# Second matmul's seven-product scheme with shared sums, and the second value pass of an attention pair begun with its shared last rows

## The chip, the cores and the metric

One NeuronCore of one Trainium2 chip runs the whole program. The metric is device time in microseconds: the median of three runs. The profile is one further execution, taken with the hardware profiler.

## The reference

```python
# q, k, v: (8 batches, 12 heads, 448 tokens, 64), float32
scores = q @ k.T / sqrt(64)
attn = exp(scores - max);  attn = attn / sum(attn)
x = (attn @ v) as (8*448 = 3584 tokens, 12*64 = 768)
h = x @ w_in            # w_in: 768 x 2048
g = h * sigmoid(h)      # silu
out = g @ w_out         # w_out: 2048 x 768 -> 3584 x 768 float32
```

## The kernel before

**Attention.** The twelve heads of a batch are three groups of four (HG = 4). A unit is one group of one batch; batch 0 is cut into two pieces of tokens. Seven units are worked alone, the other 20 as ten pairs (`ns` has two entries). A unit's keys are four chunks; in a pair the first three chunks have 128 rows each and the fourth has 64 rows of either unit, so that both units share one exponential tile, `E[(ns[0], 3)]`: its rows 0 to 63 are the first unit's last keys, rows 64 to 127 the second's. TensorE makes the scores (line 327, tile geometry 32 rows x 128 columns, in the shared chunk 32 x 64), ScalarE the exponentials (line 364), and TensorE multiplies by the values in two passes, `attend(ns, 1)` and `attend(ns, 2)` (line 390), one for each half of the head's 64 channels. Geometry there is 128 x 32, four heads side by side; for the shared chunk, called the rest, it is 64 x 32, eight matmuls side by side. Each pass of a pair is seven steps: three for each unit, and then the rest. The sums of the exponentials are part 0 (`attend_sums`, line 406). VectorE's `norm` (line 473) divides and frees the two banks of a pass.

**First matmul.** `ffn1` (line 487) makes h in 16 blocks of 128 hidden units for a batch; ScalarE's tanh (line 498) and VectorE's gate (line 534) make G. The last two batches go together through a seven-product scheme of their own (`pair_product`, line 623, with sums on VectorE at lines 581 and 599), which the change leaves alone.

**Second matmul.** The 28 tiles of 128 tokens are 14 quads of two tiles, a and b. The first quad is done plainly (line 709). Each of the other 13 is a 2 x 2 block product: rows are the two token tiles, the inner dimension is the two halves of the hidden units, columns the two halves of 768. Seven products of eight 128x128x384 matmuls (line 695) take the place of eight. `combine_w` (line 524) makes sums of w_out's quarters once, in halves; `combine_g` (line 685) makes five sums of G's quarters for each quad, in two halves each, into S tiles (a ring of NSG) or in place; `product(qd, m)` runs one product; two products may share a PSUM bank, the second added on top of the first after the first has been read. The readers are ScalarE copies (lines 753, 759, 763) and VectorE adds (line 749) of 128x384 float32, with temporaries `s` and `m` (a ring of NTMP) and output tiles `ost` (a ring of four). `store` sends an output tile out as four DMAs of 48 KB, from SP; in the last two quads two of the four go from ScalarE. `tmp`, `s`, `m`, `u` and `ost` are in SBUF; `a`, `h`, `p`, `f` and `o` banks share a ring of four PSUM banks (tag "m").

**Order.** Nothing is ordered by hand. A planner (`Order`, `run_av`, `queue_quad`, the loop at the end) walks through modelled time with a cost for each operation, and picks for TensorE the next of scores, value passes and the list `moe` whose inputs, banks and ring places are free; VectorE and ScalarE take the ready operation with the smallest due time. The program is emitted in that order, and each engine then runs its own instructions strictly in it. `SWITCH` is the planner's price for a change of TensorE's tile geometry:

```python
SWITCH = 0.094
    def on_pe(self, op, mode):
        gap = SWITCH if mode != self.mode else 0.0
```

A product's `deps()` name what must be done before it, and a ring's `take` and `give` stand for buffers; `STORE = 3.0` is the planner's time from the last write of an output tile until it is free again.

Of the kernel before, what the change touches and what calls it, by code (L numbers as in the profile page):

```python
# [165 lines left out]
def kernel(  # L166
# [41 lines left out]
    NSG, NTMP, NOST = 3, 3, 4  # L208
# [11 lines left out]
    zeros = const.tile([128, 128], FP16, name="zeros")  # L220
    nc.vector.memset(zeros, 0.0)
    ones = const.tile([128, 32], FP16, name="ones")
    nc.vector.memset(ones, 1.0)
    half = const.tile([128, 2, 32], FP16, name="half")
    nc.vector.memset(half, 0.0)
    for i in range(2):
        nc.vector.memset(half[:, i, 16 * i : 16 * (i + 1)], 1.0)
# [170 lines left out]
    def attend_sums(ns):  # L398
        a = ps.tile([128, 512], FP32, name=f"a_{ns[0]}_0", tag="m", bufs=4)
        for n in ns:  # L400
            acc[(n, 0)] = a
        for i, (w, e) in enumerate(
            ((half[:, 0], T[ns[0]]), (half[:, 1], T[ns[1]]), (both, E[(ns[0], 3)]))
        ):
            for h in range(HG):
                nc.tensor.matmul(  # L406
                    out=a[32 * h : 32 * (h + 1), 0:S],
                    lhsT=w,
                    rhs=e[:, h, 0:S],
                    start=(i == 0),  # L410
                    stop=(i == 2),
                )

    def attend(ns, part):
        made = []
        lone = len(ns) == 1
        if part == 0 and not lone:
            attend_sums(ns)
            return
        for n in ns:  # L420
            a = ps.tile([128, 512], FP32, name=f"a_{n}_{part}", tag="m", bufs=4)
            made.append(a)
            acc[(n, part)] = a
# [84 lines left out]
    W_ = {m: const.tile([128, HF, OH], FP16, name=f"D{m}") for m in (1, 4, 6)}  # L508
# [5 lines left out]
    W_[3], W_[7], W_[5], W_[2] = B_[0, 1], B_[1, 0], B_[1, 1], B_[0, 0]  # L514

    def combine_w(m, f0, f1):
        i0, i1, op = {
            1: ((0, 0), (1, 1), ALU.add),
            4: ((1, 0), (0, 0), ALU.subtract),
            6: ((0, 0), (0, 1), ALU.add),  # L520
            3: ((0, 1), (1, 1), ALU.subtract),
            7: ((1, 0), (1, 1), ALU.add),
        }[m]
        nc.vector.tensor_tensor(
            out=W_[m][:, f0:f1], in0=B_[i0][:, f0:f1], in1=B_[i1][:, f0:f1], op=op
        )
# [129 lines left out]
    def first_silu():  # L656
        t = const.tile([128, 1], FP16, name="first_silu")
        nc.scalar.activation(out=t, in_=zeros[:, 0:1], func=AF.Silu)
# [11 lines left out]
    def combine_g(qd, m, f0, f1):  # L670
        a, b = 2 * qd, 2 * qd + 1
        x, y, op = {
            5: (rows(a, 0), rows(a, 1), ALU.add),
            2: (rows(b, 0), rows(b, 1), ALU.add),
            1: (rows(a, 0), rows(b, 1), ALU.add),
            6: (rows(b, 0), rows(a, 0), ALU.subtract),
            7: (rows(a, 1), rows(b, 1), ALU.subtract),
        }[m]
        if m > 5:
            dst = x  # L680
# [4 lines left out]
        nc.vector.tensor_tensor(out=dst[:, f0:f1], in0=x[:, f0:f1], in1=y[:, f0:f1], op=op)  # L685

    BANK = {3: 3, 5: 3, 4: 4, 2: 4, 1: 1, 7: 1, 6: 6}

    def product(qd, m):
        w = {3: rows(2 * qd, 0), 4: rows(2 * qd + 1, 1), 6: rows(2 * qd + 1, 0), 7: rows(2 * qd, 1)}  # L690
# [34 lines left out]
    def tmp(qd, name):  # L725
        tmp_t[(qd, name)] = sb.tile([128, OH], FP32, name=f"{name}_{qd}", tag="tmp", bufs=NTMP)
        return tmp_t[(qd, name)]
# [24 lines left out]
    def take_3(qd):  # L752
        nc.scalar.copy(out=tmp(qd, "s"), in_=bank(qd, 3))

    def take_4(qd):
        add(tmp_t[(qd, "s")], bank(qd, 4), tmp_t[(qd, "s")])

    def take_5(qd):
        nc.scalar.copy(out=ost(qd, 0, 1), in_=bank(qd, 3))  # L759
        store(qd, 0, 1)  # L760

    def take_2(qd):
        nc.scalar.copy(out=ost(qd, 1, 0), in_=bank(qd, 4))  # L763
        store(qd, 1, 0)

    def take_1(qd):
        add(tmp(qd, "m"), bank(qd, 1), tmp_t[(qd, "s")])

    def less_12(qd):
        add(tmp_t[(qd, "s")], tmp_t[(qd, "s")], ost_t[(qd, 0, 1)], ALU.subtract)  # L770

    def less_21(qd):
        add(tmp_t[(qd, "m")], tmp_t[(qd, "m")], ost_t[(qd, 1, 0)], ALU.subtract)

    def take_6(qd):
        add(ost(qd, 1, 1), bank(qd, 6), tmp_t[(qd, "m")])
        store(qd, 1, 1)

    def take_7(qd):
        add(ost(qd, 0, 0), bank(qd, 1), tmp_t[(qd, "s")])  # L780
        store(qd, 0, 0)
# [104 lines left out]
    pr_op, sg_op, w_op, plain_op = {}, {}, {2: [], 5: []}, {}  # L886
# [3 lines left out]
    def queue_ffn1(b, g0, g1):  # L890
        t0, t1 = 32 * g0, 32 * g1
        for f in range(NFF) if b == 0 else [x for f in range(HF) for x in (f, f + HF)]:
# [22 lines left out]
            def deps(f=f):  # L915
# [3 lines left out]
                for qd in range(NT * B // 4) if u else ():  # L919
                    if any(t // NT == u - 1 and (r or t % NT < 4) for t in (2 * qd, 2 * qd + 1)):  # L920
                        made += (
                            [plain_op.get(x) for x in ((0, 0), (0, 1), (1, 0), (1, 1))]
                            if qd == 0
                            else [pr_op.get((qd, m)) for m in (3, 4, 6, 7)]
                        )
# [55 lines left out]
    def queue_pair_f(f, xs):  # L981
        done, lo = {}, f // 4 * 4

        def free(r):
            made = []
            for qd in range(NT * B // 4):
                for t in (2 * qd, 2 * qd + 1):
                    if t // NT == PB // 2 - 1 and t % NT < (4, NT - 1)[r]:
                        made += [pr_op.get((qd, m)) for m in (3, 4, 6, 7)]
# [68 lines left out]
    def sums_w(ms):  # L1058

        for m in ms:  # L1060
            w_op[m] = [
# [5 lines left out]
                        ld_wout + list(plain_op.values()) * (m in (3, 7)),  # L1067
# [6 lines left out]
    def queue_plain(t, j):  # L1074
# [6 lines left out]
        def queue(f0, f1):  # L1081
            def run():
# [10 lines left out]
                if len(plain_op) == 4:  # L1093
                    sums_w((3, 7))
# [22 lines left out]
    def plan_sums():  # L1117
# [12 lines left out]
        for m in (5, 2, 1, 6, 7):  # L1130
            sg_op[(qd, m)] = []
            for f0 in (0, 4):
                deps = [x for f in range(f0, f0 + 4) for x in gates[f] + gates[f + HF]]
                if m > 5:
                    deps += sg_op[(qd, {6: 2, 7: 5}[m])]
# [12 lines left out]
    def queue_quad(qd):  # L1148
# [3 lines left out]
        def read(m, eng, fn, deps, then=None):  # L1152
            if m in (5, 2):
                then = lambda at: (m_ring.give(at), ost_ring.give(at + STORE))
            elif m in (6, 7):
                then = lambda at: (
                    m_ring.give(at), ost_ring.give(at + STORE), tmp_ring.give(at)
                )
# [4 lines left out]
        def queue(m, first):  # L1163
            def run():
# [5 lines left out]
                if m in (5, 2, 1):  # L1170
# [3 lines left out]
                if m == 3:  # L1174
                    read(3, "ACT", take_3, [op])
                elif m == 4:
                    read(4, "DVE", take_4, [op, took[3]])
                elif m == 5:
                    read(5, "ACT", take_5, [op], m_ring.give)
                elif m == 2:  # L1180
                    read(2, "ACT", take_2, [op], m_ring.give)
                elif m == 1:
                    read(1, "DVE", take_1, [op, took[4]])
                    read("less_12", "DVE", less_12, [took[1], took[5]])
                    read("less_21", "DVE", less_21, [took[1], took[2]])
                elif m == 6:
                    read(6, "DVE", take_6, [op, took["less_21"]], m_ring.give)
                else:
                    read(7, "DVE", take_7, [op, took["less_12"]], m_ring.give)

            def deps():
                made = list(w_op.get(m, [None])) + [x for y in first if y for x in [took.get(y)]]
                if m in (3, 4):
                    t = 2 * qd + m - 3
                    for b in {(128 * t + c) // S for c in (0, 127)}:
                        for f in range(HF):
                            x = g_op.get((b, f + HF * (m - 3)), [None])
                            made += [(y, f * mm(OH)) for y in x]
                    return made + ld_wout
                if m in (1, 6, 7):  # L1200
                    made += [pr_op.get((qd, x)) for x in ((5, 2) if m == 1 else (1,))]
# [3 lines left out]
            rings = {3: ((tmp_ring, 1),), 1: ((tmp_ring, 1),), 4: ()}  # L1205
            rings = rings.get(m, ((ost_ring, 1),))
            moe.append((deps, 1 if BANK[m] == m else 0, run, rings))


        for m, first in ((3, ()), (4, (3,)), (5, (3,)), (2, (4,)), (1, ()), (6, ()), (7, (1,))):  # L1210
            queue(m, first)

    def after_x(n):
# [16 lines left out]
        if b == 0:  # L1230
            sums_w((1, 4, 6))
# [153 lines left out]
    def run_av():  # L1385
# [27 lines left out]
        od.on_pe(op, "cols")  # L1413
        if two and part:
            od.mode = "rest cols"
# [140 lines left out]
```

## Time and profile before

| | |
|---|---|
| median of 3 runs | 395.43 us (395.18 to 395.46) |
| the profiled execution's own time | 395.72 us |
| its span | 393.9 us |
| TensorE | 386.8 us busy, 98% of the span, 3679 matmuls |
| VectorE | 311.0 us, 79%, 653 instructions |
| ScalarE | 243.1 us, 62%, 378 instructions |
| granted TensorE clock | 1.00 |
| second matmul's sums of G, line 685 | 130 instructions, about 0.42 us each |
| its reading adds on VectorE, line 749 | 78 instructions, about 0.55 us each |
| its copies on ScalarE, lines 753, 759, 763 | 39 instructions, 0.48 us each |
| sums of w_out, line 524 | 10 instructions, about 0.94 us each |
| stores, line 744 | 224 DMAs of 48 KB, median 1.7 us from issue to landing |

A matmul's duration in the profile includes its way through the array, and matmuls overlap; how long one holds TensorE is read from the distance between starts. The same holds in part for VectorE and ScalarE, whose next instruction can begin before the last one's end.

### The profile page before, as it was taken

The page shows a single profiled execution, that of the slowest core. Times are in us where ns is not written, and L with a number is a line of the kernel's source. Part 1 is how long each engine was busy: PE and PEld are TensorE (multiplying, and loading weights), DVE is VectorE, ACT ScalarE, POOL GpSimd, SP SyncE. Part 2 cuts the span into 40 slices and gives each one's busy share as a digit, 9 for nine tenths or more (in the row PEclk, how much of TensorE's full clock was granted, in tenths as well). Part 3 has the DMA queues.
Part 4 walks back from the last instruction along what each step waited for, and adds up shares of the span by engine and source line. Part 5 has one row for each costly group of instructions (what it writes and reads, how often), then busy time and mean ns, then how long its engine had stood idle before and what let it go on. Part 6 is the DMA issues. An engine that isn't in the chain of part 4 may idle for free.

```text
span 393.9 us, 9299 instructions
## 1 busy us (share of the span) xinstructions
PE 386.8 (98%) x3679; PEld 199.3 (51%) x3679; DVE 311.0 (79%) x653; ACT 243.1 (62%) x378; POOL 83.7 (21%) x153
## 2 busy tenths in 40 slices
PE   7999999999999999999999999999999999999995
PEld 6667774443444444544444444344444555556563
DVE  2476676999999697896888886988879898786863
ACT  4988885696863878626868529687593227872110
POOL 6632447205003232500051221500000000000000
PEclk9999999999999999999999999999999999999999
DMA  7999999919034863582134861801100131001334
GB/s 112 203 210 210 164 177 185 162 35 142 0 71 95 140 95 47 77 157 70 25 48 78 143 108 47 119 2 42 42 1 2 40 81 40 2 1 42 80 82 121
DMA packets 35580, 34.44 MB, mean 87 GB/s; under 512 B 11600, under 2 KB 34000, under 8 KB 35536
## 3 DMA queue, kind: packets, MB, share of 16 engines
q0 software_dynamic: 24784, 22.82, 38.7%
q1 hardware_dynamic: 9984, 10.24, 9.5%
q10 hardware_dynamic: 768, 0.79, 0.8%
q8 instruction: 29, 0.48, 0.5%
q14 instruction: 15, 0.12, 0.1%
HBM read 45.61 MB, written 11.01 MB: 144 GB/s over the span
## 4 chain that ended last, share of the span: by engine, by line
PE 96%; DMA 1%; ACT 1%; issue 0%; DVE 0%; POOL 0%; POOLq 0%
PE p L695 31%; PE h L487 29%; PE s L327 13%; PE a L390 10%; PE f L623 8%; PE o L709 3%; PE a L406 2%; DMA rq<-in_q_dram 1%; PE z L1463 1%; ACT E L364 1%; POOL rk L248 0%; DVE ost L749 0%; ACT ost L763 0%; DVE rq L314 0%; ACT th L498 0%
## 5 line engine op out<-in xcount | busy, mean ns | idle before, releaser
L364 ACT ACTIVATE E<-s 128x896 f16<-128x896 f32 (+1 forms) x172 | 149.9, 915 | 48.9 <-PE s L327 47.7
L487 PE MATMUL h<-xT,w_in_t 128*128 128x448 f16 (+1 forms) x672 | 118.5, 327 | 0.0
L487 PEld LDWEIGHTS <-w_in_t 128*128 128x128 f16 x672 | 61.2, 98 | 54.1 <-issue 18.0
L498 ACT ACTIVATE th<-h 128x448 f16<-128x448 f32 (+1 forms) x112 | 54.2, 494 | 31.4 <-PE h L487 22.5
L534 DVE SCALAR_TENSOR_TENSOR G<-th,h 128x448 f16<-128x448 f16 (+2 forms) x112 | 55.4, 509 | 16.0 <-ACT th L498 13.7
L269 POOL DMA_DIRECT2D V<-in_v_dram x88 | 48.6, 571 | 57.4 <-PE a L390 43.8
L327 PE MATMUL s<-rq,KT 32*128 32x448 f16 (+4 forms) x864 | 56.7, 340 | 1.4 <-DVE rq L314 0.9
L695 PEld LDWEIGHTS <-G 128*128 128x128 f16 x384 | 36.5, 98 | 28.1 <-issue 4.4
L695 PEld LDWEIGHTS <-S 128*128 128x128 f16 x312 | 29.3, 98 | 23.8 <-issue 5.2
L390 PE MATMUL a<-E,V 128*32 128x448 f16 (+3 forms) x864 | 40.4, 335 | 0.0
L695 PE MATMUL p<-D,G 128*128 128x384 f16 x208 | 37.6, 326 | 0.0
L695 PE MATMUL p<-w_out_t,S 128*128 128x384 f16 x208 | 37.1, 326 | 0.0
L254 POOL DMA_DIRECT2D rq<-in_q_dram x27 | 15.2, 561 | 103.2 <-PE s L327 83.8
L473 DVE SCALAR_TENSOR_TENSOR xT<-a,rdn 128x448 f16<-128x448 f32 (+1 forms) x54 | 28.8, 567 | 7.3 <-PE a L390 6.4
L327 PEld LDWEIGHTS <-KT 32*128 32x128 f16 (+2 forms) x864 | 17.5, 98 | 29.5 <-issue 26.0
L695 PE MATMUL p<-w_out_t,G 128*128 128x384 f16 x176 | 31.9, 326 | 0.0
L390 PEld LDWEIGHTS <-V 128*32 128x32 f16 (+2 forms) x864 | 18.2, 95 | 22.4 <-issue 14.7
L375 DVE TENSOR_TENSOR T<-T,E 128x1792 f16<-128x1792 f16 x20 | 21.8, 1090 | 8.3 <-ACT E L364 8.1
L685 DVE TENSOR_TENSOR S<-G 128x512 f16<-128x512 f16 x70 | 25.4, 416 | 3.2 <-PE p L695 3.0
L375 DVE TENSOR_TENSOR T<-E,E 128x1792 f16<-128x1792 f16 x20 | 21.7, 1084 | 5.8 <-ACT E L364 5.8
L759 ACT COPY ost<-p 128x384 f32<-128x384 f32 x13 | 6.2, 480 | 26.9 <-PE p L695 22.1
L304 DVE STREAM_TRANSPOSE KT<-rk 128x256 f32<-128x256 f32 (+3 forms) x48 | 16.6, 384 | 6.4 <-DMA rk<-in_k_dram 5.7
(72 smaller groups left out, 364.1 us busy)
## 6 DMA issues: line engine op xcount, KB each, us to landing
out_dram<-ost SPq DMA_DIRECT2D x208, 48.0 KB, 1.7
rk<-in_k_dram POOLq DMA_DIRECT2D x24, 224.0 KB, 5.7
rq<-in_q_dram POOLq DMA_DIRECT2D x21, 224.0 KB, 5.2
w_in_t<-in_moe_w_in_dram POOLq DMA_DIRECT2D x6, 512.0 KB, 11.4
w_out_t<-in_moe_w_out_dram POOLq DMA_DIRECT2D x4, 768.0 KB, 12.9
V<-in_v_dram POOLq DMA_DIRECT2D x43, 64.0 KB, 3.9
V<-in_v_dram POOLq DMA_DIRECT2D x40, 48.0 KB, 3.8
out_dram<-ost ACTq DMA_DIRECT2D x16, 48.0 KB, 1.8
```

What stands on the lines that cost most here:

```text
L269: nc.gpsimd.dma_start(out=VT[b][32 * x : 32 * (x + 1), hs, 0:count, :], in_=v[b, hs].rearrange("h (i g) d -> i h g d", g=TPP)[:, :, first ...
L327: nc.tensor.matmul(out=pS[p0 : p0 + 32 * (x1 - x0), h % 2, at : at + nq], lhsT=KT[(b, hg)][32 * h : 32 * (h + 1), c, x0:x1, :, e], rhs=QT[ ...
L364: nc.scalar.activation(out=E[(n, w)][0:kr, 2 * y : 2 * y + 2, 0:nk], in_=pS_t[(n, w, y)][0:kr, :, 0:nk], func=AF.Exp, scale=attn_scale,)
L375: nc.vector.tensor_tensor(out=T[n], in0=T[n] if step else E[(n, 0)], in1=E[(n, step + 1)], op=ALU.add,)
L390: nc.tensor.matmul(out=a[32 * h : 32 * (h + 1), 0:nq], lhsT=w, rhs=e[k0:k1, h, at : at + nq], start=start, stop=stop,)
L473: nc.vector.scalar_tensor_tensor(out=x3(b, cc)[:, cc % 3, 32 * g0 : 32 * g1], in0=acc[(n, part)][:, 0:nq], scalar=0.5, in1=rdn_t[n].rearra ...
L487: nc.tensor.matmul(out=h[:, 0 : t1 - t0], lhsT=w_in_t[:, cc, 128 * f : 128 * (f + 1)], rhs=x3(b, cc)[:, cc % 3, t0:t1], start=(cc == 0), s ...
L498: nc.scalar.activation(out=th, in_=h_t[(b, f, t0)][:, 0 : t1 - t0], func=AF.Tanh)
L534: nc.vector.scalar_tensor_tensor(out=dst[:, f, at + lo : at + hi], in0=th_t[(b, f, t0)][:, lo - t0 : hi - t0], scalar=1.0, in1=h_t[(b, f, ...
L623: nc.tensor.matmul(out=pp_t[(f, PBANK[m])], lhsT=w[:, c, :], rhs=a[:, c, :], start=(c == 0 and m in (1, 6, 5, 7)), stop=(c == 2), skip_gro ...
L685: nc.vector.tensor_tensor(out=dst[:, f0:f1], in0=x[:, f0:f1], in1=y[:, f0:f1], op=op)
L695: nc.tensor.matmul(out=pr_t[(qd, BANK[m])][:, 0:OH], lhsT=w[:, f, :], rhs=W_[m][:, f, :], start=(f == 0 and BANK[m] == m), stop=(f == HF - 1),
```

## The change

1. The seven products are those of another scheme. With a, b the token tiles and 0, 1 the halves: S5 = b0 + b1, S6 = S5 - a0, in place b0 := a0 - b0 (for product 7), S3 = a1 - S6; four sums for each quad instead of five, in a chain. Weights: four sums instead of five, also a chain (B11 - B01, + B00, then B10 less that, and in place B01 - B00). Products run in the order 1, 6, 2, 7, 5, 4, 3 instead of 3, 4, 5, 2, 1, 6, 7. Bank 1 takes products 1 and 2, bank 7 products 7 and 4, bank 5 products 5 and 3, product 6 has its own.
2. The readers: ScalarE copies product 1 into `u` and bank 1 (with product 2) out; VectorE makes five adds, all of which read a bank. It was three ScalarE copies and six adds, of which two read SBUF alone.
3. NSG is 4 instead of 3, NTMP 2 instead of 3; `zeros` lies in an S tile, `half` and `ones` are views of one tile, `first_silu` writes into a `th` tile.
4. In a pair, part 2 begins with the rest (64 x 32) and then runs the three chunks of either unit (128 x 32); part 1 still ends with the rest. The planner's mode follows.

Core of the diff (resource declarations and ring bookkeeping cut):

```diff
-    NSG, NTMP, NOST = 3, 3, 4
+    NSG, NTMP, NOST = 4, 2, 4
...
     def attend(ns, part):
...
+        def rest():
+            for h in range(HG):
+                for i, n in enumerate(ns):
+                    attend_mm(
+                        acc[(n, part)], n, part, 3, h, 64 * i, 64 * (i + 1), E[(ns[0], 3)],
+                        part == 2, part == 1,
+                    )
+
+        if part == 2 and not lone:
+            rest()
+        for n in ns:
             for c in range(NCH if lone else NCH - 1):
                 for h in range(HG):
                     attend_mm(
-                        a, n, part, c, h, 0, rows_of(n, c), E[(n, c // per_burst(n))],
-                        c == 0, lone and c == NCH - 1,
+                        acc[(n, part)], n, part, c, h, 0, rows_of(n, c),
+                        E[(n, c // per_burst(n))],
+                        c == 0 and (lone or part == 1),
+                        c == NCH - 1 or (c == NCH - 2 and not lone and part == 2),
                     )
-        if not lone:
-            for h in range(HG):
-                for i, n in enumerate(ns):
-                    attend_mm(
-                        made[i], n, part, 3, h, 64 * i, 64 * (i + 1), E[(ns[0], 3)],
-                        False, True,
-                    )
+        if part == 1 and not lone:
+            rest()
...
-            1: ((0, 0), (1, 1), ALU.add),
-            4: ((1, 0), (0, 0), ALU.subtract),
-            6: ((0, 0), (0, 1), ALU.add),
-            3: ((0, 1), (1, 1), ALU.subtract),
-            7: ((1, 0), (1, 1), ALU.add),
+            3: (B_[1, 1], B_[0, 1], ALU.subtract),
+            2: (W_[7], B_[0, 0], ALU.add),
+            4: (B_[1, 0], W_[6], ALU.subtract),
+            1: (B_[0, 1], B_[0, 0], ALU.subtract),
...
-            5: (rows(a, 0), rows(a, 1), ALU.add),
-            2: (rows(b, 0), rows(b, 1), ALU.add),
-            1: (rows(a, 0), rows(b, 1), ALU.add),
-            6: (rows(b, 0), rows(a, 0), ALU.subtract),
-            7: (rows(a, 1), rows(b, 1), ALU.subtract),
+            5: (rows(b, 0), rows(b, 1), ALU.add),
+            6: (S_t.get((qd, 5)), rows(a, 0), ALU.subtract),
+            7: (rows(a, 0), rows(b, 0), ALU.subtract),
+            3: (rows(a, 1), S_t.get((qd, 6)), ALU.subtract),
...
-    BANK = {3: 3, 5: 3, 4: 4, 2: 4, 1: 1, 7: 1, 6: 6}
+    BANK = {1: 1, 2: 1, 6: 6, 7: 7, 4: 7, 5: 5, 3: 5}
...
+    def take_1(qd):
+        nc.scalar.copy(out=tmp(qd), in_=bank(qd, 1))
+    def take_2(qd):
+        nc.scalar.copy(out=ost(qd, 0, 0), in_=bank(qd, 1))
+        store(qd, 0, 0)
+    def take_6(qd):
+        add(tmp_t[qd], bank(qd, 6), tmp_t[qd])
+    def take_7(qd):
+        add(ost(qd, 1, 1), bank(qd, 7), tmp_t[qd])
+    def take_5(qd):
+        add(ost_t[(qd, 1, 1)], bank(qd, 5), ost_t[(qd, 1, 1)])
+        store(qd, 1, 1)
+    def take_4(qd):
+        add(ost(qd, 1, 0), bank(qd, 7), tmp_t[qd])
+        store(qd, 1, 0)
     def take_3(qd):
-        nc.scalar.copy(out=tmp(qd, "s"), in_=bank(qd, 3))
...
+        add(ost(qd, 0, 1), bank(qd, 5), tmp_t[qd])
         store(qd, 0, 1)
...
+                made += [took.get(y) for y in {2: (1,), 4: (7,), 3: (5,)}.get(m, ())]
+                made += [(pr_op.get((qd, y)), 9.0) for y in {6: (1,), 7: (6,), 5: (7,), 3: (4,)}.get(m, ())]
...
-        for m, first in ((3, ()), (4, (3,)), (5, (3,)), (2, (4,)), (1, ()), (6, ()), (7, (1,))):
-            queue(m, first)
+        for m in (1, 6, 2, 7, 5, 4, 3):
+            queue(m)
...
-        od.on_pe(op, "cols")
+        od.on_pe(op, "rest cols" if two and part == 2 else "cols")
         if two and part:
-            od.mode = "rest cols"
+            od.mode = ("rest cols", "cols")[part - 1]
```

More of the change, by code (lines that the diff above doesn't have):

```diff
@@ L218 @@
     )
-    zeros = const.tile([128, 128], FP16, name="zeros")
+    zeros = sb.tile([128, NFF // 2, 128], FP16, name="zeros", tag="S", bufs=NSG)[:, 0]
     nc.vector.memset(zeros, 0.0)
-    ones = const.tile([128, 32], FP16, name="ones")
+    cols = const.tile([128, 64], FP16, name="cols")
+    ones, half = cols[:, 16:48], (cols[:, 32:64], cols[:, 0:32])
+    nc.vector.memset(cols, 0.0)
     nc.vector.memset(ones, 1.0)
[L224 to L227, printed above, removed]
     both = const.tile([128, 32], FP16, name="both")
@@ L402, in attend_sums @@
         for i, (w, e) in enumerate(
-            ((half[:, 0], T[ns[0]]), (half[:, 1], T[ns[1]]), (both, E[(ns[0], 3)]))
+            ((half[0], T[ns[0]]), (half[1], T[ns[1]]), (both, E[(ns[0], 3)]))
         ):
@@ L420, in attend @@
         for n in ns:
-            a = ps.tile([128, 512], FP32, name=f"a_{n}_{part}", tag="m", bufs=4)
-            made.append(a)
-            acc[(n, part)] = a
+            acc[(n, part)] = ps.tile([128, 512], FP32, name=f"a_{n}_{part}", tag="m", bufs=4)
+        def rest():
[8 more added lines that the diff above has]
+        for n in ns:
             for c in range(NCH if lone else NCH - 1):
@@ L507 @@
     X = const.tile([128, NFF, 128], FP16, name="X")
-    W_ = {m: const.tile([128, HF, OH], FP16, name=f"D{m}") for m in (1, 4, 6)}
+    W_ = {m: const.tile([128, HF, OH], FP16, name=f"D{m}") for m in (2, 3, 4)}
     B_ = {
@@ L656, in first_silu @@
     def first_silu():
-        t = const.tile([128, 1], FP16, name="first_silu")
-        nc.scalar.activation(out=t, in_=zeros[:, 0:1], func=AF.Silu)
+        t = sb.tile([128, S], FP16, name="first_silu", tag="th", bufs=3)[:, 0:1]
+        nc.scalar.activation(out=t, in_=both[:, 0:1], func=AF.Silu)
     def silu(f, r, x):
@@ L723, in bank, with tmp @@
         return pr_t[(qd, m)][:, 0:OH]
-    def tmp(qd, name):
-        tmp_t[(qd, name)] = sb.tile([128, OH], FP32, name=f"{name}_{qd}", tag="tmp", bufs=NTMP)
-        return tmp_t[(qd, name)]
+    def tmp(qd):
+        tmp_t[qd] = sb.tile([128, OH], FP32, name=f"u_{qd}", tag="tmp", bufs=NTMP)
+        return tmp_t[qd]
     def ost(qd, i, j):
@@ L749, in add @@
         nc.vector.tensor_tensor(out=out, in0=a, in1=b, op=op)
-    def take_3(qd):
-        nc.scalar.copy(out=tmp(qd, "s"), in_=bank(qd, 3))
[L755 to L759, printed above, removed]
-        store(qd, 0, 1)
[L762 to L781, printed above, removed]
+    def take_1(qd):
[13 more added lines that the diff above has]
+        store(qd, 1, 0)
+    def take_3(qd):
+        add(ost(qd, 0, 1), bank(qd, 5), tmp_t[qd])
+        store(qd, 0, 1)
     units = []
@@ L923, in deps @@
                             if qd == 0
-                            else [pr_op.get((qd, m)) for m in (3, 4, 6, 7)]
+                            else [pr_op.get((qd, m)) for m in (1, 2, 4, 7)]
                         )
@@ L988, in free @@
                     if t // NT == PB // 2 - 1 and t % NT < (4, NT - 1)[r]:
-                        made += [pr_op.get((qd, m)) for m in (3, 4, 6, 7)]
+                        made += [pr_op.get((qd, m)) for m in (1, 2, 4, 7)]
             return made
@@ L1060, in sums_w @@
         for m in ms:
-            w_op[m] = [
+            out = {1: 5, 2: 6, 3: 7, 4: 4}[m]
+            w_op[out] = [
                 od.add(
@@ L1066, in sums_w @@
                         lambda m=m, f0=f0: combine_w(m, f0, f0 + 4),
-                        ld_wout + list(plain_op.values()) * (m in (3, 7)),
+                        ld_wout
+                        + [w_op[x][f0 // 4] for x in {2: (7,), 4: (6,)}.get(m, ())]
+                        + list(plain_op.values()) * (m == 1),
                         30,
@@ L1129, in plan_sums @@
         sg_ring.take(3)
-        for m in (5, 2, 1, 6, 7):
+        for m in (5, 6, 7, 3):
             sg_op[(qd, m)] = []
@@ L1161, in read, with out, both, queue @@
             took[m] = od.add(Op(eng, busy, lambda: fn(qd), deps, bias, then=then))
-        def queue(m, first):
+        def out(at):
+            ost_ring.give(at + STORE)
+        def both(*rings):
+            return lambda at: [m_ring.give(at), out(at)] + [r.give(at) for r in rings]
+        def queue(m):
             def run():
@@ L1173, in run @@
                 pr_op[(qd, m)] = op
-                if m == 3:
-                    read(3, "ACT", take_3, [op])
-                elif m == 4:
[L1177 to L1187, printed above, removed]
+                if m == 1:
+                    read(1, "ACT", take_1, [op])
+                elif m == 6:
+                    read(6, "DVE", take_6, [op, took[1]], m_ring.give)
+                elif m == 2:
+                    read(2, "ACT", take_2, [op], both())
+                elif m == 7:
+                    read(7, "DVE", take_7, [op, took[6]])
+                elif m == 5:
+                    read(5, "DVE", take_5, [op, took[7]], out)
+                elif m == 4:
+                    read(4, "DVE", take_4, [op, took[6]], both())
@@ L1188, in run @@
                 else:
-                    read(7, "DVE", take_7, [op, took["less_12"]], m_ring.give)
+                    read(3, "DVE", take_3, [op, took[4]], both(tmp_ring))
             def deps():
-                made = list(w_op.get(m, [None])) + [x for y in first if y for x in [took.get(y)]]
-                if m in (3, 4):
-                    t = 2 * qd + m - 3
+                made = list(w_op.get(m, [None]))
+                made += [took.get(y) for y in {2: (1,), 4: (7,), 3: (5,)}.get(m, ())]
@@ L1199, in deps @@
                     return made + ld_wout
-                if m in (1, 6, 7):
-                    made += [pr_op.get((qd, x)) for x in ((5, 2) if m == 1 else (1,))]
                 x = sg_op.get((qd, m), [None, None])
                 return made + [x[0], (x[1], 4 * mm(OH))]
-            rings = {3: ((tmp_ring, 1),), 1: ((tmp_ring, 1),), 4: ()}
-            rings = rings.get(m, ((ost_ring, 1),))
-            moe.append((deps, 1 if BANK[m] == m else 0, run, rings))
-        for m, first in ((3, ()), (4, (3,)), (5, (3,)), (2, (4,)), (1, ()), (6, ()), (7, (1,))):
-            queue(m, first)
+            rings = {1: ((tmp_ring, 1),), 2: ((ost_ring, 1),), 7: ((ost_ring, 1),)}
@@ L1213, in after_x @@
+            rings.update({4: ((ost_ring, 1),), 3: ((ost_ring, 1),)})
+            rings = rings.get(m, ())
+            moe.append((deps, int(BANK[m] == m), run, rings))
+        for m in (1, 6, 2, 7, 5, 4, 3):
+            queue(m)
     def after_x(n):
```

38 lines of the change are left out of this document (16 added, 22 removed).

## Prediction

> **What bounds the kernel now.** I read the page first, then TensorE's waits, then the chain of waits in order of time, then the timeline around the two places where TensorE stood still beside the changed code, and last the output tiles' own view.
>
> ```profile
> span 393.9 us, 9299 instructions
> PE 386.8 (98%) x3679; PEld 199.3 (51%) x3679; DVE 311.0 (79%) x653; ACT 243.1 (62%) x378; POOL 83.7 (21%) x153
> ...
> PE 96%; DMA 1%; ACT 1%; issue 0%; DVE 0%; POOL 0%; POOLq 0%
> ```
>
> TensorE carries 96% of the chain. VectorE's 79% and ScalarE's 62% are not the bound, so work taken off them counts only where TensorE waits for them. All of TensorE's waits:
>
> ```profile
> PE z L1463 <- DVE zeros L221: 1.0, 1, 1.0
> PE s L327 <- DVE rq L314: 0.9, 1, 0.9
> PE p L695 <- ACT ost L763: 0.6, 1, 0.6
> PE s L327 <- ACT E L364: 0.4, 1, 0.4
> PE a L390 <- issue: 0.2, 1, 0.2
> ```
>
> Only the third lies in code that the change touches. So the time is nearly the sum of TensorE's steps, and the chain shows what a step costs:
>
> ```profile
> 75.91 2.27 PE h L487 x12
> ...
> 78.69 2.38 PE h L487 x12
> ...
> 120.90 3.13 PE a L390 x61
> 124.03 1.41 PE p L695 x8
> ...
> 156.16 1.30 PE p L695 x8
> ```
>
> Columns are start, length, what. Twelve h matmuls take 2.27 us behind work of the same tile geometry (0.189 each) and 2.38 behind scores: a change of geometry costs about 0.1. A product is 1.30 without, 1.41 with. The two value passes of a pair, back to back, are 14 steps of 0.189, or 2.65, yet take 3.13: four changes (128x32 to 64x32, back, again, and out) are the other 0.48. (x61 for 64: a few records are missing.)
>
> **The geometry changes.** The matmul count stays 3679 with the same shapes, so the steps cost the same. I counted the changes over the two built orders: 258 before, 251 after. A change's price is the distance from a step's first start to the next step's first start in this trace, less the step's own columns (0.187 for 448: the 0.189 above, of which 0.002 is what every step adds); within a kind it varies by a few ns. By kind, with C for 128x32, R for the 64x32 rest, F for full 128x128, S for the scores' 32x128:
>
> - C to R, 20 to 10, at 0.106: -1.06. R to F, 13 to 4, at 0.129: -1.16. F to C, 13 to 6, at 0.096: -0.67. S to F, 59 to 56, at 0.109: -0.33.
> - C to F, 12 to 22, at 0.108: +1.08. R to C, 6 to 10, at 0.127: +0.51. S to C, 28 to 31, at 0.105: +0.32.
> - New kinds: F to R, 5, for which the trace has no row; the nearest are F to the scores' 32x64 step at 0.096 and C to R at 0.106, so +0.48 to +0.53. R to R across two passes, 5, no change of geometry; bounds are C to C at 0.003 and one 32x64 step behind another at 0.041 (eight staggered starts, which is the nearer row), so +0.02 to +0.20; a gain below nothing is excluded, since no step is shorter than its columns.
>
> Sum -0.58 to -0.82; with 0.096 and 0.03 for the new kinds it is -0.69. Only five of the ten pairs have their passes back to back in the new order; for the others the change moves a geometry change from one pass to the other.
>
> The Trainium skill (TensorEngine Tiling (Array Packing), Tiling Modes) says that changing the tiling mode, but not merely the tile, drains TensorE; it gives no price. The trace agrees for mode changes, with 0.096 to 0.129; no row here yet shows R to R. If the drain were the 128 cycles that the skill's TensorE: Matmul & The Clock Gate (Part 2) names, an estimate of 0.053 us at 2.4 GHz, seven changes fewer would be 0.37 us instead of 0.69, and the time 394.8.
>
> Beginning part 2 with the rest needs both accumulators at its first step instead of the second one three steps (0.57) later. The planner takes both banks before it starts either way, and TensorE shows no wait of a value pass for VectorE, so I cost that at nothing; without that cover it is at most 0.57 a pair.
>
> **The readers and sums.** Start to start in runs of their own kind, a G sum takes 0.33 (six in 2.06, below), a reading add 0.47, a w_out sum 0.87, a ScalarE copy 0.51. Off VectorE: 26 x 0.33 + 13 x 0.47 + 2 x 0.87 = 16.4 us; back on it 29 wait-only instructions at about 0.035 (the gap in front of dependent work in the timeline), 1.0. Off ScalarE: 13 x 0.51 = 6.6. All this hides under TensorE and is worth nothing by itself. It matters at the two stalls:
>
> ```profile
> 221.77 2.06 DVE L685 TENSOR_TENSOR S<-G 128x512 f16<-128x512 f16 x6
> ...
> 222.38 2.97 PE L695 MATMUL p<-w_out_t,S 128*128 128x384 f16 x16
> ...
> 309.38 0.48 ACT L763 COPY ost<-p 128x384 f32<-128x384 f32 x1 [2.27 <-PE p L695]
> 309.91 1.46 PE L695 MATMUL p<-D,S 128*128 128x384 f16 x8 [0.57 <-ACT ost L763]
> ```
>
> At 222.4 sixteen matmuls last 2.97; elsewhere sixteen last 2.76. In between, product 5 of quad 6 reached its fifth matmul, whose half of S came fourth of the six sums: 0.19 stood still, behind a q transpose that had waited 1.0 for its load. In the new order S5's two halves stand next to each other, and product 1, which needs no sum, goes first. I take the 0.19 as gone (bounds: gone, or still there).
>
> At 309.2, product 1 of quad 8 needs a bank and all four are held; it waits for ScalarE's copy: from the last product's last start, 0.73 more than a step. After the change the copy is no longer what frees a bank there. By the new VectorE order the two norms of the last value pass stand behind a 0.78 sum of x and two 0.91 sums of w_in, as now: 0.2 (TensorE's tail) + 0.78 + 1.82 + 0.62 (first norm) + 0.05 = 3.4 us after that pass, while TensorE has one change and two products, 2.7, before it needs the norm's bank. So a stall of about 0.7 stays in place of 0.73, on VectorE instead of ScalarE: -0.05. Bounds: 0 if the sums start later than the norms, 1.2 if the second norm is needed too.
>
> Waits that the change adds: product 4 waits for `take_7`, product 3 for `take_5`, both on VectorE, 2 for `take_1` on ScalarE; before, 5 waited for ScalarE, 2 and 7 for VectorE. Number and distance are the same, one product between: 1.30 less 0.2 tail, 0.55 add, 0.05 hop leaves 0.5. Behind a waiting VectorE read stand the next sums and norms. In the last four quads nothing longer than another read stands in front.
>
> The end: the last product is read by one VectorE add and four stores, as now (390.01 add, then 2.0 to the last landing). Three stores 1.3 apart instead of two come before; on SP and ScalarE two issues of 0.46 each fit into 1.3. Cost 0, bounds -0.1 and +0.2. The start has two memsets fewer, beside a load that takes 4 us: nothing.
>
> **Sum.** -0.69 - 0.19 - 0.05 = -0.93. The profiled execution, 395.72, would become 394.79; it stands 0.29 over the median, so the median goes from 395.43 to 394.5. About 0.2%, or 0.8 us, is what a measurement here can tell from no change; 394.64 is that border, so the forecast lies just beyond it.
>
> **Rivals.**
>
> *Stores hold VectorE (slower).* Three of a quad's four output tiles are now first written by VectorE, and `take_7` gates product 4. If the tile's old store has not landed, VectorE's queue stands, and TensorE behind it.
>
> ```profile
> L744 SPq DMA_DIRECT2D out_dram<-ost x208: 314/419/2017, 65.6 to 391.1; - x104
> ...
>   DMA out_dram<-ost: 10.1, 4
> ...
> DMA to landing us min/median/max: 1.5/1.7/6.7
> ```
>
> Engines waited 10.1 us for stores, 9.1 of it on ScalarE, which cost TensorE nothing that I can find. From a tile's last write to its last store's landing I read 1.9 to 8.8 us from the store queues' packets; 5.5 at most in the last 40 us, where SP's four issues at 0.46 fill 1.9 of each store. In the new order the (1,1) tile is free for six products less the add, 7.2 us (5.9 once). It decides where a store lands more than 7.7 after its write (7.2 plus the 0.5 of slack); at 8.8, 1.1 each, for two late quads +2.2 on the forecast: 396.7.
>
> *Reads come late on VectorE (slower).* Five of seven bank reads are there instead of four. Three misjudged waits of 0.6 each, where a 1.09 T sum stands in front: 396.3. Against it: 15.4 us net come off VectorE, and it made TensorE wait in only one place of this code before. The Trainium skill (TensorEngine Tiling (Array Packing), Performance Considerations) speaks for this rival: it wants both ScalarE and VectorE to empty PSUM.
>
> *No change that can be measured.* The geometry term is at its small end and the 0.19 comes back at another sum: 395.43 - 0.58 = 394.85; with one new stall of 0.5, 395.35. For it: five of ten pairs gain nothing inside their passes, and every order shift can move a wait.
>
> *More gain.* The norms come ahead of the sums around 309 and the 0.7 goes as well: 393.8. VectorE's lighter queue speaks for it, the built order against it.
>
> **How the numbers follow.** Forecast 0.50, more gain 0.10: faster 0.60. No measurable change 0.28. Stores 0.07 and late reads 0.05: slower 0.12. The range runs from the larger gain, 393.8, to 395.5, the no-change case with one stall; it leaves out the slower cases.
>
> **What would show it.** Right: in the chain, back-to-back value passes of about 3.02 instead of 3.13 (five changes' worth over the whole kernel), single passes still 1.56; TensorE busy to about 389.0 of a span of 393.0; no doubled step near 220; a stall of about 0.7 near 309 behind VectorE's norm; about 269 VectorE tensor-tensor instructions for 310. Wrong: passes of 3.13 (the prices are not additive), TensorE waiting for `ost` adds or for stores in the last 40 us, or a new wait for the G sums in quads 1 to 9.

## The result and the profile after

The changed kernel takes 394.45 us, median of 15 runs; the kernel before, run beside it, 395.6. The ratio is 0.9971, with a 95% interval of 0.9963 to 0.9979: 1.15 us faster, the interval from 0.8 to 1.5. The forecast was 394.5, 0.93 faster. The profiled execution went from a span of 393.9 to 393.0. Here and below, single slow runs, 3.5% and more longer than the rest of their kernel's, count in the medians but not in the ratios, and the ratios aren't those of the medians.

The page and all of TensorE's waits:

```profile
span 393.0 us, 9255 instructions
PE 386.6 (98%) x3679; PEld 199.7 (51%) x3679; DVE 296.2 (75%) x610; ACT 238.7 (61%) x365; POOL 83.7 (21%) x153
...
PE 94%; DMA 2%; DVE 1%; ACT 1%; issue 0%; POOL 0%; SPq 0%; ACTq 0%; DVEq 0%; POOLq 0%
```

```profile
PE z L1459 <- DVE cols L224: 1.0, 1, 1.0
PE p L696 <- DVE xT L477: 0.5, 1, 0.5
PE s L325 <- ACT E L362: 0.4, 1, 0.4
PE a L388 <- issue: 0.2, 1, 0.2
PE s L325 <- DVE rq L312: 0.2, 1, 0.2
```

VectorE lost 14.8 us of busy time and ScalarE 4.4 (15.4 and 6.6 were worked out), and neither shows in the time by itself; TensorE has as many matmuls as before. In the changed code one wait is left, on VectorE's `xT` where it was on ScalarE's copy. The chain (start, length, what):

```profile
76.11 2.27 PE h L491 x12
...
78.89 2.38 PE h L491 x12
...
102.89 1.30 PE p L696 x8
...
118.26 3.00 PE a L388 x63
121.26 1.41 PE p L696 x8
```

The steps cost what they cost before: twelve h matmuls 2.27 and 2.38, a product 1.30 and 1.41. A pair's two passes back to back take 3.00 instead of 3.13.

Spans of single executions hide some of this: the first h matmul starts anywhere from 29.5 to 30.9 us in the nine profiles of this study that are compared here, with the arrival of the first loads. The table therefore gives, from the traces, the stretch from the first plain matmul of the second product (line 709 before) to the start of the last matmul, and from there to the span's end.

| kernel | changes of geometry | first plain matmul to last matmul | last matmul to end | median us | ratio to before (95%) |
|---|---|---|---|---|---|
| before | 258 | 331.30 | 4.30 | 395.6 | |
| changed | 251 | 330.32 | 4.17 | 394.45 | 0.9971 (0.9963 to 0.9979) |
| e1: value pass alone | 251 | 331.73 | 4.27 | 395.7 | 1.0004 (0.9995 to 1.0013) |
| e2: sums and readers alone | 256 | 330.99 | 4.17 | 395.16 | 0.9987 (0.9977 to 0.9996) |
| e3: norms first | 251 | 329.51 | 4.17 | 393.32 | 0.9943 (0.993 to 0.9955) |
| e4: rest in the middle | 266 | 332.11 | 4.17 | 396.17 | 1.0017 (1.0007 to 1.0026) |
| e5: more work on VectorE | 251 | 330.92 | 4.16 | 395.26 | 0.9991 (0.9982 to 1.0) |
| e6: three output tiles | 251 | 330.23 | 4.21 | 394.05 | 0.9958 (0.9943 to 0.9973) |
| e7: value pass, order of before | 252 | 330.88 | 4.29 | 394.8 | 0.9979 (0.9971 to 0.9988) |
| e8: before, three output tiles | 258 | 345.19 | 4.30 | 410.73 | 1.0389 (1.0355 to 1.0423) |

The 395.6 of before stands beside the changed kernel; beside e1 to e4 before took 395.51, and beside e5 to e8 the same. From before to changed the stretch lost 0.98 and the end 0.13.

### The profile page after: what moved, and what is told of

Read it like the earlier page. It is cut to its first block, busy times and chain, and to the rows that moved or that the text cites. A ratio compares the mean times of both kernels' runs of the same rounds, so it can differ in the third digit from the quotient of the medians.

```text
span 393.0 us, 9255 instructions
## 1 busy us (share of the span) xinstructions
PE 386.6 (98%) x3679; PEld 199.7 (51%) x3679; DVE 296.2 (75%) x610; ACT 238.7 (61%) x365; POOL 83.7 (21%) x153
## 4 chain that ended last, share of the span: by engine, by line
PE 94%; DMA 2%; DVE 1%; ACT 1%; issue 0%; POOL 0%; SPq 0%; ACTq 0%; DVEq 0%; POOLq 0%
PE p L696 29%; PE h L491 29%; PE s L325 12%; PE a L388 10%; PE f L625 8%; PE o L710 3%; PE a L404 2%; DMA rk<-in_k_dram 2%; DMA out_dram<-ost 1%; PE z L1459 1%; DVE tw L601 0%; ACT E L362 0%; DVE ost L750 0%; SPq L745 0%; DVE KT L302 0%
## 5 line engine op out<-in xcount | busy, mean ns | idle before, releaser
L696 PEld LDWEIGHTS <-S 128*128 128x128 f16 x312 | 29.5, 98 | 23.8 <-issue 3.4
L696 PE MATMUL p<-w_out_t,S 128*128 128x384 f16 x208 | 38.1, 326 | 0.5 <-DVE xT L477 0.5
L750 DVE TENSOR_TENSOR ost<-p,u 128x384 f32<-128x384 f32 x39 | 21.6, 555 | 19.4 <-PE p L696 15.5
```

What stands on the lines that cost most here:

```text
L696: nc.tensor.matmul(out=pr_t[(qd, BANK[m])][:, 0:OH], lhsT=w[:, f, :], rhs=W_[m][:, f, :], start=(f == 0 and BANK[m] == m), stop=(f == HF - 1),
L750: nc.vector.tensor_tensor(out=out, in0=a, in1=b, op=op)
```

## The experiments

### e1: the value pass alone

The kernel before with the new `attend` and, in `run_av`, the new mode:

```diff
-        od.on_pe(op, "cols")
+        od.on_pe(op, "rest cols" if two and part == 2 else "cols")
         if two and part:
-            od.mode = "rest cols"
+            od.mode = ("rest cols", "cols")[part - 1]
```

> The kernel before with the new value pass alone: part 2 of a pair begins with the rest, the planner's mode follows; sums, products and readers stay as before. Geometry changes counted over the built order: 251 (258 before); priced by kind with the rows of the trace of before, -0.86 us. Theory (TensorE's time is the sum of its steps and its geometry changes; the sums matter only at stalls): both stalls of before stay (0.19 near 222, 0.73 near 309), so 0.8 to 0.9 us faster than before, 394.7. Rival (the gain came from the work taken off VectorE and ScalarE): no change, 395.6. A new wait by the shifted order would show as a doubled step in the trace.

Measured: 395.7, no change. My expectation was missed by 1.0 us, and at first sight the rival's number is the one that came out. The trace tells where the gain went. TensorE's timeline of e1, and of before at the same scores:

```profile
113.42 0.56 PE L406 MATMUL a<-T,half 128*32 128x448 f16 x8
113.81 0.36 PE L406 MATMUL a<-E,both 128*32 128x448 f16 x4
114.49 0.37 PE L327 MATMUL s<-rq,KT 32*128 32x448 f16 x2 [0.32 <-ACT E L364]
115.30 0.57 PE L327 MATMUL s<-rq,KT 32*128 32x448 f16 x6 [0.44 <-ACT E L364]
```

```profile
114.62 0.36 PE L406 MATMUL a<-E,both 128*32 128x448 f16 x4
114.91 1.47 PE L695 MATMUL p<-w_out_t,S 128*128 128x384 f16 x8
116.22 1.46 PE L695 MATMUL p<-D,G 128*128 128x384 f16 x8
117.62 0.57 PE L327 MATMUL s<-rq,KT 32*128 32x448 f16 x8
```

Before, two products stand between the sums of a pair and the next scores; with the new mode the planner puts the scores right behind the sums, where the two score banks are still being read by ScalarE's exponentials. Start to start, the steps around 114 us last 1.23 more than their columns and their changes of geometry. The stall near 222 stayed, and is 0.30 here instead of 0.19. The -0.86 that I expected of the geometry counts nothing for the six places where a rest now stands behind a rest. At the 0.013 that this trace shows for them, and with R to C at 0.121 (mean of ten here) instead of 0.127, it is -0.84. With the waits, +1.23 and +0.11, that makes +0.50; the stretch in the table is 0.43 longer. So seven changes fewer don't show in e1's time because an order shift took more than they gave. e7 takes that shift away.

### e7: the value pass with the order of before

The kernel before with the new `attend` alone; `run_av` as it was, so the planner orders everything as before.

> The kernel before, part 2 of a pair begun with the rest, but the planner told nothing: its order is that of the kernel before, instruction for instruction, except inside the second passes. 252 geometry changes; by kind -0.76 us with 0.03 for two rests in a row, -0.65 to -0.81 with the bounds. Theory (the gain of the value pass is real, and in the run of that part alone it was lost to the wait for exponentials near 114 us, 1.23, which the planner's order made): no such wait here, 394.8 with before at 395.5. Rival (beginning with the rest costs in the pass what it saves): 395.5.

Measured: 394.8, ratio 0.9979: 0.7 faster, as expected, and no wait near 114. The working behind the expectation was off, though: -0.76 is the sum with nothing for the six rests behind a rest, not with 0.03 for each, which gives -0.58. At their measured 0.013, and R to C at 0.121, it is -0.74. The stretch lost only 0.42, because two steps near 220 and 222 last 0.15 and 0.34 longer (0.19 before): as I read it, TensorE reaches the sums of quad 6 earlier and VectorE is no earlier. -0.74 + 0.30 = -0.44. The profiled execution, 395.32, is the slowest of the eleven runs; the other 0.3 of the 0.7 isn't explained by its trace. With the order held, the value pass gains what its geometry says.

### e2: the sums, products and readers alone

The changed kernel with the `attend` and the mode of before.

> The changed kernel with the old value pass (rest last in both passes, the planner's mode as before): the sums, products, readers and rings alone. Geometry changes counted: 256; by kind -0.20 us against before. Theory: 0.19 near 222 gone, 0.73 near 309 become 0.68 to 0.70, so 0.4 us faster than before, 395.2, hardly to be told from no change. Rival (work off VectorE is the gain): about 0.9 to 1.0 faster, 394.6. The two parts add up to the whole (-0.86 - 0.4 = -1.3 against -1.15 measured) only if the order shifts of the two do not overlap.

Measured: 395.16, ratio 0.9987 with an interval of 0.9977 to 0.9996, so barely faster. The rival's 394.6 is just the lower end of that interval, so the time alone leans against it, and the trace decides. In it nothing lasts longer near 222; the step near 309 lasts 0.74 more; the stretch is 0.31 shorter, of which the geometry is 0.20 and the stall near 222 is 0.19, less 0.12 for a new wait of product 2 of quad 10 (the changed kernel has it too). The end is 4.17 instead of 4.30, as in every kernel with the new readers (e1 and e7, with the old, have 4.27 and 4.29).

### e4: the rest in the middle of part 2

```diff
-        if part == 2 and not lone:
-            rest()
         for n in ns:
+            if part == 2 and not lone and n == ns[1]:
+                rest()
```

(The start and stop flags follow.)

> The changed kernel with the rest of part 2 in the middle, between the first and the second unit's chunks; the order of everything else is untouched, the matmuls are the same. 266 geometry changes instead of 251. Theory (each change of geometry holds TensorE for 0.096 to 0.129 us wherever it stands): by kind +1.6 to +1.7 us against the changed kernel, 396.1. Rival (a change hides under the neighbouring steps' waits, or costs the 0.053 that the drain estimate gave): +0 to +0.8, 394.5 to 395.3.

Measured: 396.17, against 394.45 for the changed kernel: +1.7; the stretch is 1.79 longer. For 15 changes more, that is 0.12 each. The chain shows it pass by pass:

```profile
118.44 3.24 PE a L388 x64
...
166.08 1.56 PE a L388 x32
171.65 1.68 PE a L388 x32
```

Back to back 3.24 instead of 3.00, two changes; apart, the second pass 1.68 instead of 1.56, one. The changes of geometry cost what the rows said, and add up.

### e3: the norms ahead of the sums

In the planner, the rule that holds VectorE back for an urgent operation, wider for the sums of x and w_in alone:

```diff
-                if urgent < self.now + self.shy * best[1].busy:
+                if urgent < self.now + (1.2 if best[1].bias in (4, 8) else self.shy) * best[1].busy:
```

> The changed kernel; the planner's rule that holds back VectorE work for an urgent operation waits longer when the work held back is a sum for the last two batches' seven-product scheme (1.2 instead of 0.5 of its length), so that the two norms of the last value pass come ahead of the sums of x and w_in. 251 geometry changes, as in the changed kernel. Theory: the 0.70 stall near 309 goes and nothing takes its place: 0.7 faster than the changed kernel, 393.8, 1.7 faster than before. Rival: the sums come late for the products of the last two batches and TensorE waits there instead: no faster than the changed kernel, 394.5.

Measured: 393.32, ratio 0.9943, the fastest of all here. Timelines of the changed kernel and of e3:

```profile
307.15 0.86 DVE L583 TENSOR_TENSOR sx<-xT,xT 128x1344 f16<-128x1344 f16 x1 [0.95 <-PE a L388]
307.93 1.82 DVE L601 TENSOR_TENSOR tw<-w_in_t 128x1536 f16<-128x1536 f16 x2
...
309.67 1.15 DVE L477 SCALAR_TENSOR_TENSOR xT<-a,rdn 128x448 f16<-128x448 f32 x2
...
310.34 1.47 PE L696 MATMUL p<-w_out_t,S 128*128 128x384 f16 x8 [0.53 <-DVE xT L477]
```

```profile
305.43 1.82 DVE L601 TENSOR_TENSOR tw<-w_in_t 128x1536 f16<-128x1536 f16 x2
...
307.17 1.15 DVE L477 SCALAR_TENSOR_TENSOR xT<-a,rdn 128x448 f16<-128x448 f32 x2
...
308.96 1.46 PE L696 MATMUL p<-w_out_t,S 128*128 128x384 f16 x8
```

In the changed kernel the norms, which free the banks of the last value pass, stand behind three sums that nobody needs yet; the product in want of a bank starts 0.70 late. In e3 two of the sums use VectorE's idle time ahead of the norms, the third comes after, and the product starts on time. No wait took its place: the stretch is 0.81 shorter than in the changed kernel, 0.70 for this stall and 0.10 for a wait of product 2 of quad 10 (353.9 us in the changed kernel, below) that is gone too. The medians differ by 1.1; the 0.3 that the trace doesn't show lies within the two intervals.

### e5: work put back on VectorE

```diff
-        nc.vector.tensor_tensor(out=dst[:, f0:f1], in0=x[:, f0:f1], in1=y[:, f0:f1], op=op)
+        for _ in range(2 if m == 5 and qd < 13 else 1):
+            nc.vector.tensor_tensor(out=dst[:, f0:f1], in0=x[:, f0:f1], in1=y[:, f0:f1], op=op)
...
-        add(ost(qd, 0, 1), bank(qd, 5), tmp_t[qd])
+        t = ost(qd, 0, 1)
+        for _ in range(2 if qd < 13 else 1):
+            add(t, bank(qd, 5), tmp_t[qd])
```

> The changed kernel with work put back on VectorE that the planner doesn't know of: in quads 1 to 12 both halves of S5 are summed twice and the last reading add is made twice. 24 x 0.33 + 12 x 0.47 = 13.6 us more on VectorE, nearly the 15.4 that the change took off. Theory (the relief of VectorE is worth nothing by itself): TensorE waits only where VectorE is busy without a gap, between 306 and 320 us; there at most one more wait of 0.8, so 394.5 to 395.3. Rival (the relief is the gain): all of the 1.15 is lost, 395.6, with waits in several quads between 105 and 303 us.

Measured: 395.26, at the upper end of what the theory allowed. The ratio's interval, 0.9982 to 1.0, ends at the time of before, so the time alone hardly excludes the rival; its waits in several quads are what the trace can show. From the first plain matmul on, the trace has one new wait of more than 0.1 us:

```profile
311.96 1.67 DVE L687 TENSOR_TENSOR S<-G 128x512 f16<-128x512 f16 x4
...
313.56 0.55 DVE L751 TENSOR_TENSOR ost<-p,ost 128x384 f32<-128x384 f32 x1
...
314.16 1.46 PE L697 MATMUL p<-w_out_t,S 128*128 128x384 f16 x8 [0.47 <-DVE ost L751]
```

Product 3 of quad 8 waits for `take_5`, behind the doubled sums of quad 9: 0.64 start to start, and the stretch is 0.60 longer. Between 105 and 303 us, where the attention's VectorE work runs and more than half of the added work falls, TensorE lost nothing. So, as far as this run puts work back, VectorE's relief is worth something only in the stretch around 310 us where its queue has no gap.

### e6 and e8: one output tile fewer

```diff
-        t = sb.tile([128, OH], FP32, name=f"ost_{qd}_{i}{j}", tag="ost", bufs=NOST)
+        t = sb.tile([128, OH], FP32, name=f"ost_{qd}_{i}{j}", tag="ost", bufs=3)
```

In the changed kernel:

> The changed kernel with three buffers for output tiles instead of four; the planner still counts four, so the order is the same. Theory (stores have room): a tile is free for about 5 us, one store (1.9 of issue and 1.7 of landing) fits, VectorE's queue stands at times but TensorE has 0.5 of slack: 394.5 to 395.2. Rival (output tiles written by VectorE are the weak point of the change): every late store stands on TensorE's path, 1 to 2 us in each of the last four quads, 398 or more.

In the kernel before:

> The kernel before with three buffers for output tiles instead of four; the planner still counts four, so the order is the same. It tells what the four buffers are worth to the old readers: there the two tiles that ScalarE writes are read again by VectorE (less_12, less_21) after product 1, three products later, and are held 4 us longer. Theory: the old scheme needs its four buffers more than the new one: at least 3 us slower than before, 398.5 or more, against at most 0.7 for the changed kernel. Rival (the new readers are the ones at risk): this one no slower than 0.5, 396.0.

Measured: 394.05 for the changed kernel, no slower than with four, and from the first plain matmul on no wait of TensorE that it didn't have. The kernel before with three tiles takes 410.73, 15 us more; the direction was expected, the size was not. Its VectorE and TensorE at the longest of the waits for an output tile:

```profile
235.74 0.56 DVE L749 TENSOR_TENSOR ost<-p,s 128x384 f32<-128x384 f32 x1 [4.04 <-DMA out_dram<-ost]
```

```profile
236.35 1.84 PE L390 MATMUL a<-E,V 128*32 128x448 f16 x32 [3.14 <-DVE ost L749]
238.13 2.74 PE L695 MATMUL p<-D,G 128*128 128x384 f16 x8
```

VectorE stood 4.0 us for a store, and TensorE 3.1 behind it: the mechanism of my first rival is real, but it belongs to the old readers. The code says why, as I read it: they hold two output tiles as operands of `less_12` and `less_21` until after product 1, and the new ones read no output tile that has been stored.

## Why the prediction was right, point by point

- **Geometry, -0.69.** The changed trace has rows for the two new kinds. Full array to rest: 0.096, the value taken. Rest to rest across two passes: 0.013, where I took 0.03 and called the 32x64 row at 0.041 the nearer; the row at 0.003 was. With these the sum is -0.77. R to C, 0.127 in the trace of before, is 0.122 on average over the ten of the changed trace, which makes it -0.82. e4 prices the changes independently at 0.12 each. The back-to-back passes came to 3.00; 3.02 was said.
- **Drain.** Rest to rest at 0.013, beside 0.12 for each change that e4 adds, shows that it is the change of mode that costs. The Trainium skill (TensorEngine Tiling (Array Packing), Tiling Modes) says so of the drain: a change of tiling mode drains TensorE, a change of tile alone doesn't. The estimate of 0.053 that I had worked out from the Trainium skill (TensorE: Matmul & The Clock Gate, Part 2) doesn't fit: by it e4 would have been 0.8 slower, and it was 1.8 slower in the trace.
- **The stall near 222, -0.19.** Gone in the changed kernel and in e2; still there, and longer, in e1 and e7, which lack the new sums. The products on S there in the changed kernel, each as long as a product elsewhere:

```profile
221.06 1.46 PE L696 MATMUL p<-w_out_t,S 128*128 128x384 f16 x8
...
225.93 1.47 PE L696 MATMUL p<-w_out_t,S 128*128 128x384 f16 x8
```

- **The stall near 309, -0.05.** 0.70 instead of 0.73, behind the norms, as worked out from the queue; e3 shows the queue to be the cause. That the size came out so well is partly luck: the terms added up there make 3.47, not 3.4, and would have given a stall of 0.77.
- **Added waits at nothing.** Nearly: product 2 of quad 10 waits once for `take_1`, which stands behind a silu on ScalarE, 0.10:

```profile
352.93 0.58 ACT L663 ACTIVATE G<-v 128x448 f16<-128x448 f32 x1 [0.79 <-DVE v L656]
...
353.41 0.46 ACT L754 COPY u<-p 128x384 f32<-128x384 f32 x1
...
353.92 1.46 PE L696 MATMUL p<-w_out_t,X 128*128 128x384 f16 x8
```

- **The end at nothing.** It is 0.13 shorter, just beyond my bound of 0.1. VectorE's last two adds, before and after:

```profile
389.19 0.56 DVE L749 TENSOR_TENSOR ost<-p,m 128x384 f32<-128x384 f32 x1
390.01 0.56 DVE L749 TENSOR_TENSOR ost<-p,s 128x384 f32<-128x384 f32 x1 [0.26 <-PE p L695]
```

```profile
387.92 0.56 DVE L750 TENSOR_TENSOR ost<-p,u 128x384 f32<-128x384 f32 x1 [0.74 <-PE p L696]
389.22 0.56 DVE L750 TENSOR_TENSOR ost<-p,u 128x384 f32<-128x384 f32 x1 [0.74 <-DMA out_dram<-ost]
```

  Before, the last two output tiles were ready 0.82 apart, while ScalarE needs 0.85 to issue a store's two DMAs and SP 0.78. So the last store began 0.09 (SP) and 0.16 (ScalarE) after its add had ended, where 0.03 is what the store before it took. Now the tiles are 1.30 apart and the last store begins after 0.03; from the last add's end to the last landing it is 2.26 instead of 2.39. That there is room I had worked out for after, but not that there had been none before.
- **The sum.** -0.82 - 0.19 - 0.03 + 0.10 - 0.13 = -1.07, against 1.11 less in the trace (0.98 and 0.13) and 1.15 in the medians. The forecast of 0.93 fell short by the prices of rest to rest and of R to C and by the end; the new wait offset a part.
- **The rivals.** Stores: in the changed kernel's trace ScalarE waits 14.2 us for stores and VectorE 2.7, and no wait of TensorE follows from it; e6 is against it too. Late reads: TensorE waits for none of VectorE's five adds, though the Trainium skill (TensorEngine Tiling (Array Packing), Performance Considerations) wants both engines to empty PSUM; two of seven reads on ScalarE were enough here. More gain: not in this order, but e3 shows that the gain it named was there to be had. What I gave as the forecast's weakness, that every order shift can move a wait, decided e1.

What stays open: I haven't split e3's 0.3 beyond its trace, nor e7's, from the scatter of the runs.

## What to carry to other kernels

Where one engine's chain is 96% of the span, count its steps and its mode changes in the built order and price each kind by start-to-start distances: that gave this change to 0.2 us, while 15 us taken off VectorE gave little by themselves. A part measured alone can show nothing and still be worth its price, when a planner's order shifts with it; run it once more with the order held fixed. Look for work that nobody needs yet in front of the operation that frees a bank: sums moved out of the way of two norms were worth 0.8 us in the trace, nearly as much as the whole change.

## What the runs showed of the hardware

After the 3.1 us wait in e8 (233.2 to 236.4 us), TensorE came back at full clock and lost half of it 1.2 us later. Its windows (PE, weight loads, VectorE, ScalarE, GpSimd, then the granted clock, the DMA share and GB/s):

```profile
230.00:237.00 7.00, 3.86 (x58) 1.91 (x60) 2.85 (x7) 0.48 (x1) 0.00 (x0) 1.00 0.27 70
237.00:239.00 2.00, 2.00 (x27) 0.72 (x20) 1.90 (x5) 0.00 (x0) 0.44 (x1) 0.63 0.40 104
239.00:241.00 2.00, 2.00 (x10) 0.75 (x12) 1.78 (x5) 0.00 (x0) 2.00 (x5) 0.52 0.54 54
241.00:244.00 3.00, 3.00 (x26) 1.41 (x22) 1.61 (x3) 1.73 (x3) 0.30 (x1) 1.00 1.00 147
```

The 0.63 and 0.52 are means over windows that reach beyond the slow stretch. Cut more finely, the granted clock is 1.00 from 236.3 to 237.4, 0.50 from 237.5 to 240.9, and 1.00 from 241; the slow stretch is 3.41 us long. The eight matmuls of the product in it last 2.74 instead of 1.46, so that product alone lost 1.3 us on top of the wait.

That the wait brought this on is not shown. The same execution has a wait of 3.3 us (328.1 to 331.4, on ScalarE), and the clock is 1.00 all through the four microseconds after it; so it is after a wait of 2.2 us that ends at 126.0. A reading that fits all three, and that no run here tests: the clock is judged once in every 3.41 us, in a fixed raster that can be counted from 237.52, where the slow stretch begins. Then the 3.1 us wait left 2.2 us of one interval idle, while the 3.3 us wait fell into two intervals with 1.6 and 1.7 and the 2.2 us wait into two with 1.1 each. The Trainium skill (TensorE: Matmul & The Clock Gate, Part 1) describes a gate that halves the clock after an idle window of about 3.4 us; this run agrees with the half, and shows it where TensorE had stood for less than that. In the kernels near the change, whose waits in the table's stretch are 1.2 us and less, the granted clock over the profile is 0.998 or more.
